# Down of two token blocks by seven half products: an attention and SwiGLU layer on one core

## The chip, the core and the metric

The kernel runs on one core of a Trainium2 chip. Five engines work side by side, each through its own list of instructions in order: TensorE (PE) multiplies matrices, VectorE (DVE) and ScalarE (ACT) work on rows, GpSimd (POOL) does little here, and SyncE (SP) issues nearly all DMA transfers. Semaphores order them where one needs another's result. The metric is the device time of one execution in microseconds (us), as the median of several runs.

## What is computed

`x` is 2048 tokens of 640 features, fp32. The reference, cut to what matters:

```python
q, k, v = (layernorm(x) @ wqkv) split into 32 heads of 20
logits  = q[s] . k[s - 2*w] * 20**-0.5  for w = 0..7      # sliding window of 8, step 2
h       = x + (softmax(logits) @ v) @ wo
g, u    = silu(layernorm(h) @ w_gate), layernorm(h) @ w_up    # 640 -> 1728
out     = h + (g * u) @ w_down                            # 1728 -> 640
```

Gate and Up are the products with `w_gate` and `w_up`; Down is the one with `w_down`.

## The kernel before

The 2048 tokens are four blocks of 512 (numbered 0 to 3 in the code; here the first to the fourth), each of four tiles of 128 rows. Every fp32 product is made of three products of a faster format: each operand is split into a high part (a cast on ACT) and the low rest (a subtraction on DVE), and high x high, low x high and high x low are added up in one of eight banks of 128 x 512 in PSUM. The 1728 features of the feed-forward part are 14 F-tiles, the last of 64.

The program runs in stages that overlap. The projection to q, k, v (L580) of the blocks comes first; attention itself is DVE and ACT work with transfers through DRAM, spread over more than half of the span; the output projection `wo` (L827, matmuls of 320 columns) follows block by block. The first two blocks then run gate and up (L899, banks 5 and 6), and Down (L910): the four tiles of rows go into banks 0 to 3, 512 of the 640 output columns wide, and the other 128 columns, turned, into bank 4. `finish` copies bank 4 (L1197), turns it back by four transposes on TensorE (L1201), and adds the results to h (L1209, L1212).

The third and fourth block share gate and up: F-tiles p and p+6 form a pair, the two blocks are the other dimension, and the 2 x 2 product of halves is done by seven products in place of eight (L994, added up on DVE at L1137). `early` does what needs the third block alone, `pair` the rest: 78 matmuls a pair, in banks 5, 6 and 7. F-tiles 12 and 13 stay plain (L1016). Down of these two blocks is ordinary: each tile's 15 matmuls are put between the products of the next pair, and the third block's F-tiles p+6, kept until then (`stash`), are done at the end (`closing`).

Before gate and up stands a second norm, whose result must be turned so that features lie on partitions. Half of the columns of the first three blocks go by DVE transposes and a transfer out and back, the other half by TensorE (L447, added at L450); the fourth block goes by DVE and DRAM alone (L455, L457 to a DRAM tensor `ysc`, L463 back, L472).

Nothing of the order on an engine follows from the order of the code. Each operation is recorded with an engine, a guessed cost and a priority (`P.add`). `order` schedules the list several times (`ROUNDS`), each time with due times worked back from the round before, and sorts by start time; a table `SHIFT` moves single operations by so many microseconds. Each engine then issues its operations in that sequence, SP its transfers.

The head: DVE makes the statistics of the first tiles (L390 to L392), TensorE turns them (L541), ACT casts the columns (L543) and the weights (L554), DVE makes the low parts (L544, L556).

## Time and profile before

| what | value |
|---|---|
| median of 3 runs | 841.8 us (841.59 to 842.68) |
| the profiled execution | 841.39 us |
| its span, first to last instruction | 839.3 us |
| granted TensorE clock | 0.999 |
| ACT busy | 414.0 us, 49% |
| DMA moved | 198.32 MB, 236 GB/s |

The span is what the profile divides up; the 2.1 us between it and the run's time lie around the program. A row of a group gives the line, engine and operation, the tiles written and read, the shape and the count, then the busy time in us, the mean of one in ns, and the idle time ahead of them with what ended it. A matmul's own duration overlaps the next, so what one costs in a stream is read from stretches of them. A row of a stretch gives, for each engine, busy us and instructions, then the clock, the DMA share and GB/s.

### The profile page before, as it was taken

The numbers are of one execution on the slowest core, as the hardware profiler recorded it, in microseconds if no ns is written. First come the engines' busy times: TensorE is split into PE (matmuls) and PEld (weight loads), VectorE is DVE, ScalarE is ACT, GpSimd is POOL, SyncE is SP. The second block draws the span as 40 slices with busy tenths as digits, with TensorE's granted clock in tenths as the row PEclk, the third lists the DMA queues.
The fourth block names the chain that finished last, engine by engine and source line by source line (L and its number), as shares of the span: only waits on it lengthen the run. The fifth ranks groups of instructions, "written<-read, shape, count | busy, mean of one in ns | idle before, by whom it ended". The sixth has DMA issues, their size and how long they took to land.

```text
span 839.3 us, 10718 instructions
## 1 busy us (share of the span) xinstructions
PE 831.4 (99%) x3903; PEld 705.0 (84%) x3903; DVE 694.7 (83%) x823; ACT 414.0 (49%) x694; POOL 23.2 (3%) x33
## 2 busy tenths in 40 slices
PE   8999999999999999999999999999999999999998
PEld 7888888889978889888888988888887888888886
DVE  8599999999999999999999999996327866655552
ACT  7755853333763445755443486464465533323231
POOL 0000000000000000000000000000000000000000
PEclk9999999999999999999999999999999999999999
DMA  8996786568688687669898658787587644454441
GB/s 265 331 367 219 284 272 216 185 213 307 197 304 263 224 289 258 212 210 372 287 365 289 233 174 304 250 269 268 156 264 270 218 170 137 136 169 144 154 133 71
DMA packets 101796, 198.32 MB, mean 236 GB/s; under 512 B 35744, under 2 KB 61152, under 8 KB 101104
## 3 DMA queue, kind: packets, MB, share of 16 engines
q1 hardware_dynamic: 101744, 197.65, 69.6%
q8 instruction: 30, 0.49, 0.2%
q14 instruction: 22, 0.18, 0.1%
HBM read 147.87 MB, written 49.75 MB: 235 GB/s over the span
## 4 chain that ended last, share of the span: by engine, by line
PE 75%; DVE 15%; DMA 4%; issue 2%; ACT 2%; SPq 1%; DVEq 0%; ACTq 0%
PE bank L580 20%; PE bank L910 17%; PE bank L899 17%; PE bank L994 16%; PE bank L827 5%; DVE fa L629 2%; DVE fa L636 2%; DVE fa L672 2%; DVE fa L664 2%; DMA fa<-ysc 1%; DMA fa<-in_ffn_dram 1%; DMA ysc<-fa 1%; DVE fa L934 1%; DMA fa<-in_wqkv_dram 1%; DMA fa<-osc 1%
## 5 line engine op out<-in xcount | busy, mean ns | idle before, releaser
L899 PE MATMUL bank<-shb,ra 128*128 128x512 f32 x810 | 189.7, 390 | 1.1 <-DVE shb L450 1.1
L899 PEld LDWEIGHTS bank<-shb,ra 128*128 128x128 f32 x810 | 151.4, 188 | 32.4 <-DVE shb L450 1.5
L910 PE MATMUL bank<-ra,acts 128*128 128x512 f32 (+1 forms) x662 | 161.9, 389 | 0.2 <-DVE acts L945 0.2
L910 PEld LDWEIGHTS bank<-ra,acts 128*128 128x128 f32 x662 | 122.6, 188 | 25.5 <-DVE acts L945 0.5
L580 PE MATMUL bank<-ra,sha 128*128 128x480 f32 x480 | 105.1, 379 | 0.6 <-ACT sha L543 0.6
L580 PE MATMUL bank<-ra,shb 128*128 128x480 f32 x470 | 102.5, 378 | 0.0
L580 PEld LDWEIGHTS bank<-ra,sha 128*128 128x128 f32 x480 | 89.8, 188 | 14.5 <-ACT sha L543 0.9
L580 PEld LDWEIGHTS bank<-ra,shb 128*128 128x128 f32 x470 | 88.1, 188 | 13.2
L664 DVE TENSOR_TENSOR fa<-fa 128x2560 f32<-128x2560 f32 x32 | 90.2, 2820 | 0.6
L629 DVE TENSOR_TENSOR fa<-fa 128x2560 f32<-128x2560 f32 x32 | 90.1, 2816 | 0.8 <-DMA fa<-ksc 0.4
L636 DVE TENSOR_REDUCE fa<-fa 128x128 f32<-128x2560 f32 x32 | 90.0, 2814 | 0.4
L994 PE MATMUL bank<-shb,ra 128*128 128x512 f32 x360 | 86.8, 390 | 0.3 <-DVE fa L938 0.3
L1137 DVE TENSOR_TENSOR fa<-bank,fa 128x512 f32<-128x512 f32 x60 | 41.1, 691 | 52.8 <-PE bank L994 51.4
L994 PEld LDWEIGHTS bank<-shb,ra 128*128 128x128 f32 x360 | 67.2, 188 | 14.6 <-DVE fa L938 0.7
L672 DVE TENSOR_TENSOR fa<-fa 128x1280 f32<-128x1280 f32 (+2 forms) x70 | 76.7, 1095 | 1.1
L827 PE MATMUL bank<-ra 128*128 128x320 f32 x480 | 75.0, 310 | 0.0
L827 PEld LDWEIGHTS bank<-ra 128*128 128x128 f32 x480 | 72.1, 188 | 2.9 <-ACT fa L830 1.3
L585 ACT ACTIVATE st<-bank,fa 128x480 f32<-128x480 f32 x64 | 41.9, 656 | 57.2 <-PE bank L580 54.4
L994 PE MATMUL bank<-ra 128*128 128x512 f32 x288 | 68.2, 389 | 0.0
L944 ACT CAST acts<-fa 128x512 fp32r<-128x512 f32 x47 | 29.1, 620 | 71.9 <-DVE fa L934 50.3
L994 PEld LDWEIGHTS bank<-ra 128*128 128x128 f32 x288 | 54.1, 188 | 11.2
L876 ACT CAST ra<-fa 128x1280 fp32r<-128x1280 f32 (+1 forms) x38 | 45.8, 1205 | 24.1 <-PE bank L899 15.0
(146 smaller groups left out, 834.5 us busy)
## 6 DMA issues: line engine op xcount, KB each, us to landing
fa<-in_ffn_dram SPq DMA_DIRECT2D x46, 960.0 KB, 6.5
ra<-lsc SPq DMA_DIRECT2D x45, 320.0 KB, 3.0
fa<-ksc SPq DMA_DIRECT2D x16, 880.0 KB, 6.0
fa<-vsc SPq DMA_DIRECT2D x16, 880.0 KB, 6.9
ra<-lsc SPq DMA_DIRECT2D x21, 640.0 KB, 5.0
lsc<-ra SPq DMA_DIRECT2D x13, 640.0 KB, 3.2
ksc<-st SPq DMA_DIRECT2D x16, 320.0 KB, 2.8
qsc<-st SPq DMA_DIRECT2D x16, 320.0 KB, 3.6
```

Source lines behind the costliest of these rows:

```text
L580: T.matmul(banks[bk][:, 0:480], l, r_(wq(g, w, c), 480), start=(p, c) == first_mm, stop=(p, c) == last_mm)
L585: P.add("ACT", act(480) + 0.06, lambda bk=bk, j=j: A.activation(stage_t()[:, so : so + 1920].rearrange("p (t j c) -> p t j c", t=3, j=NJ)[ ...
L629: P.add("DVE", dve(2560), lambda: V.tensor_tensor(f(PROD, 2560).rearrange("p (j w c) -> p j w c", j=2, w=W), window(ko, 2 * jp), f(qo + 32 ...
L636: P.add("DVE", dve(2560), lambda: V.tensor_reduce(f(lo + 128 * jp, 128), f(PROD, 2560).rearrange("p (n d) -> p n d", d=DH), axis=AX.X, op= ...
L664: V.tensor_tensor(f(PROD, 2560).rearrange("p (j w d) -> p j w d", j=2, d=DH), bass.AP(tensor=fa[:, vo : vo + 160].tensor, offset=fa[:, vo ...
L672: V.tensor_add(dst(v), v[:, :, 0:m, :], v[:, :, m : 2 * m, :])
L827: T.matmul(banks[bk][:, 0:320], l, r_(m, 320), start=p == 0 and c == 0, stop=p == 2 and c == NC - 1)
L876: P.add("ACT", act(n), lambda: A.copy(r_(gu, n), f(raw, n)), r=[rf(raw, n)], w=[rr(gu, n)], prio=PR["fh"])
L899: T.matmul(banks[bk], r_(gu + 1280 * w + wid * c + col, 128), x2(a, c), start=p == 0 and c == 0, stop=p == 2 and c == NC - 1)
L910: T.matmul(banks[bk][:, lo:hi], l, m, start=first and p == 0, stop=last and p == len(passes) - 1)
L994: T.matmul(banks[bk], r_(ws[w] + 256 * q, 128), x(a, c), start=start and p == n == q == 0, stop=stop and p == 2 and n == len(terms) - 1 an ...
L1137: dv(0, lambda: V.tensor_add(fb(h, dst), banks[bk], fb(h, src)), [pb(bk)] + fr(h, src), fr(h, dst))
```

## The change

**Down of the third and fourth block.** With A11, A12 the gated F-tiles p and p+6 of the third block, A21, A22 those of the fourth, and B11 to B22 the matching halves of Down's weights (F-tile p or p+6, output columns 0 to 319 or 320 to 639), seven products P1 to P7 of 128-row tiles with 320 columns give all four quarters of the output. P1 is made in `early`, in banks 0 to 3 over all six pairs, and added to all quarters (`add_both`). The differences of weights are made on DVE after `early` (`down_combinations`), stored to DRAM with their low parts, and loaded again at the end (`turned_weights`, eight loads). A11 goes to DRAM; A21 + A22 and A22 stay on chip (`slot`), A12 as before. After the last pair `down_products` runs P4, P5, P6, P7, P2, P3, 72 matmuls each, in banks 0 to 3 and 4 to 7 by turns; DVE makes the operands' differences in place. The plain F-tiles 12 and 13 have their Down in 320 columns too.

**The norm.** TURN and HALF change: the second block's columns now go wholly by DVE and DRAM, the fourth's by TensorE (20 transposes, banks 7 and 4). `finish`, now only for the first two blocks, turns bank 4 by a DVE transpose and a transfer out and four back. Of the five small DVE operations that refine 1/sqrt, one goes to ACT, and so does a sixth that scaled the mean. `wo` of the fourth block takes banks 7 and 4.

**The head.** x's first tile comes in two halves, on SP's and ACT's queue, the other three tiles before any weight; its mean is made by ACT (256 columns) and DVE (384 columns) in `one_split`.

**The order.** ROUNDS, the priorities and SHIFT are new, the last with several hundred entries where it had fifty.

```diff
-TURN = (3,)
+TURN = (1,)
 TURNED = (3,)
-HALF = (0, 1, 2)
+HALF = (0, 2)
...
 SHIFT = {
-    26: 0.6, 31: -47, 34: -25.1, 35: -4.3, 39: -16.4, 42: 1.8, 53: -0.6, 118: 0.9, 136: -103.6, 214: 10.2, 241:
...
+    12.4, 208: 2.4, 209: -2.5, 210: 7.2, 219: 5.2, 222: 13.4, 223: -9.5, 226: -0.7, 232: -27.6, 248: 7.4, 251:
...
+            if js == (0,):
+                for a, (eng, E) in enumerate((("SP", Q), ("ACT", A))):
+                    P.add(eng, 0.4, lambda a=a, E=E: E.dma_start(
+                        fa[a:128:2, XR : XR + 640],
+                        x_in[0, 64 * a : 64 * a + 64, 0, :]), w=[("xh", a, a + 1)] if a else [rf(XR, 640)], prio=0, nbytes=nb(64, 2560))
                 return
             for j in js:
...
+                (st.one_split if j == 0 else st.one_dve if j < 3 else st.one)(j)
...
+            P.add("SP", 0.45, lambda: Q.dma_start(asc[p], f(so, 512)), r=[rf(so, 512)], w=[(f"A{p}", 0, 1)], prio=PR["js"], nbytes=nb(128, 2048))
+
+            def mm():
+                for j in range(NJ):
+                    for q, (a, w) in enumerate(((0, 0), (0, 1), (1, 0))):
+                        T.matmul(banks[j][:, 0:320], act_t()[:, ao + 512 * a + 128 * j : ao + 512 * a + 128 * j + 128], r_(dn[w], 320), start=p == q == 0, stop=p == NP - 1 and q == 2)
+            P.add("PE", 12 * 0.1475, mm, r=[("ab", ao, ao + 1024), rr(dn[0], 320), rr(dn[1], 320)], w=[pb(j) for j in range(NJ)], prio=10)
...
+        def plain_down(b, batch):
+            for n in range(2 * NJ):
+                j, o, bk = n % NJ, 320 * (n // NJ), n % 5 if b == 2 else 4
+
+                def mm(j=j, o=o, bk=bk):
+                    t = [(ao, dn, a, w) for i, ao, dn in batch for a, w in (((0, 0), (0, 1)) if i == NF - 1 else ((0, 0), (1, 0), (0, 1)))]
+                    for q, (ao, dn, a, w) in enumerate(t):
+                        T.matmul(banks[bk][:, 0:320], act_t()[:, ao + 512 * a + 128 * j : ao + 512 * a + 128 * j + 128], r_(dn[w] + o, 320), start=q == 0, stop=q == len(t) - 1)
+                P.add("PE", 5 * 0.1475, mm, r=[x for i, ao, dn in batch for x in (("ab", ao, ao + 1024), rr(dn[0], 640), rr(dn[1], 640))], w=[pb(bk)], prio=10)
+                add_row(b, j, o, bk)
+
+        def add_row(b, j, o, bk, prio=1.2):
+            row, key = hrow(b, j, o, 320)
+            P.add("DVE", dve(320), lambda: V.tensor_add(row(), banks[bk][:, 0:320], row()), r=[pb(bk), key], w=[key], prio=prio)
+
+        def add_both(b, j, bk):
+            row, key = hrow(b, j)
+            v = lambda: row().rearrange("p (h c) -> p h c", h=2)
+            P.add("DVE", dve(640), lambda: V.tensor_add(v(), banks[bk][:, 0:320][:, None, :].to_broadcast([128, 2, 320]), v()), r=[pb(bk), key], w=[key], prio=5)
```

```diff
+        def down_combinations(p):
+
+            raw, t = (PROD, SETS + 1024)[p % 2], PROD + 1280
+            for q, i in ((0, p), (1, p + NP)):
+                P.add("SP", 0.45, lambda q=q, i=i: Q.dma_start(f(raw + 640 * q, 640), ffn_in[i, :, 1280:1920]), w=rx(raw + 640 * q, 640), prio=PR["tp"], nbytes=nb(128, 2560))
+            B11, B12, B21, B22 = (raw + 320 * q for q in range(4))
+            for n, x, y in ((0, B12, B11), (1, B22, t), (2, B22, B12), (3, B21, t + 320)):
+                P.add("DVE", dve(320), lambda n=n, x=x, y=y: V.tensor_sub(f(t + 320 * n, 320), f(x, 320), f(y, 320)), r=rx(x, 320) + rx(y, 320), w=rx(t + 320 * n, 320), prio=PR["tp"])
+            for h in range(2):
+                o, src = 2048, t + 640 * h
+                P.add("ACT", act(640), lambda o=o, src=src: A.copy(act_t()[:, o : o + 640], f(src, 640)), r=rx(src, 640), w=[("ab", o, o + 640)], prio=PR["tp"])
+                P.add("DVE", dve(640), lambda o=o, src=src: V.tensor_sub(act_t()[:, o + 640 : o + 1280], f(src, 640), act_t()[:, o : o + 640].bitcast(F32)),
+                      r=rx(src, 640) + [("ab", o, o + 640)], w=[("ab", o + 640, o + 1280)], prio=PR["tp"])
+                P.add("SP", 0.45, lambda h=h, o=o: Q.dma_start(tsc[h, :, 1280 * p : 1280 * p + 1280], act_t()[:, o : o + 1280].bitcast(F32)),
...
+        def down_product(name, k, at_, bks, last=False):
+
+            ops = []
+            for p in range(NP):
+                a22, s1 = slot(2 * p + 1), slot(2 * p)
+                s2 = s1
+                src, key = {"P2": stash(p), "P3": s2, "P4": a22, "P5": s1, "P6": s2, "P7": a22}[name]
+                if name == "P6":
+                    o = SETS + 512 * p
+                    P.add("SP", 0.45, lambda p=p, o=o: Q.dma_start(f(o, 512), asc[p]), r=[(f"A{p}", 0, 1)], w=rx(o, 512), prio=PR["mld"], nbytes=nb(128, 2048))
+                    P.add("DVE", dve(512), lambda o=o, s1=s1: V.tensor_sub(s1[0](), s1[0](), f(o, 512)), r=[s1[1]] + rx(o, 512), w=[s1[1]], prio=PR["mx"])
+                if name == "P7":
+                    P.add("DVE", dve(512), lambda a22=a22, s2=s2: V.tensor_sub(a22[0](), a22[0](), s2[0]()), r=[a22[1], s2[1]], w=[a22[1]], prio=PR["mx"])
+                if name == "P3":
+                    a12 = stash(p)
+                    P.add("DVE", dve(512), lambda a12=a12, s2=s2: V.tensor_sub(s2[0](), a12[0](), s2[0]()), r=[a12[1], s2[1]], w=[s2[1]], prio=PR["mx"])
+                sp, o = RING[gn[0] % len(RING)]
+                gn[0] += 1
+                t = lambda a, n=512, c=0, sp=sp, o=o: (ra if sp == "ra" else shb)[:, o + 512 * a + c : o + 512 * a + c + n]
+                P.add("ACT", act(512), lambda t=t, src=src: A.copy(t(0), src()), r=[key], w=[(sp, o, o + 512)], prio=PR["mh"])
+                P.add("DVE", dve(512), lambda t=t, src=src: V.tensor_sub(t(1), src(), t(0).bitcast(F32)), r=[key, (sp, o, o + 512)], w=[(sp, o + 512, o + 1024)], prio=PR["ml"])
+                ws, wk = at_(p)
+                ops.append((p, t, ws, [(sp, o, o + 1024)] + wk))
```

```diff
+        def down_products():
+            low, high = (0, 1, 2, 3), (4, 5, 6, 7)
+            down_product("P4", 3, turned_weights(3, (16896, 7168)), low)
...
+            down_product("P5", 0, turned_weights(0, (0, 1920)), high)
+            for j in range(NJ):
+                add_row(2, j, 320, high[j])
+                add_row(3, j, 320, high[j])
+            down_product("P6", 1, turned_weights(1, (3840, 5760)), low)
+            for j in range(NJ):
+                add_row(2, j, 320, low[j])
+                add_both(3, j, low[j])
+            down_product("P7", 2, turned_weights(2, (7680, 9600)), high)
+            for j in range(NJ):
+                add_both(3, j, high[j])
+                store_row(3, j, 0, 640)
...
+            at_ = lambda h: lambda p: ((1280 * p + 320 * h, 1280 * p + 640 + 320 * h), [rr(1280 * p, 1280)])
+            down_product("P2", None, at_(0), low)
+            for j in range(NJ):
+                add_row(2, j, 0, low[j])
+                store_row(2, j, 0, 320)
+            down_product("P3", None, at_(1), high, last=True)
+            for j in range(NJ):
+                add_row(2, j, 320, high[j])
+                store_row(2, j, 320, 640, two=j == NJ - 1)
```

```diff
+        def finish(b):
+            so = AB2
+            P.add("ACT", act(512), lambda: A.copy(f(so, 512), banks[4]), r=[pb(4)], w=[rf(so, 512)], prio=0)
+            P.add("DVE", dve(512), lambda: V.transpose(f(so, 512), f(so, 512)), r=[rf(so, 512)], w=[rf(so, 512)], prio=PR["dt"])
+            P.add("SP", 0.45, lambda: Q.dma_start(dsc[b], f(so, 512)), r=[rf(so, 512)], w=[(f"D{b}", 0, 4)], prio=PR["dt"], nbytes=nb(128, 2048))
...
-        for i in range(2 * NP, NF):
-            step(plain(i, x2, shr))
+        plain_down(2, [plain(i, x2, shr) for i in range(2 * NP, NF)])
         for p in range(NP):
-            step(early(p), 2 if p == NP - 1 else 1)
-        wo(3, PR["w3"], (7,))
+            early(p)
+        for p in range(NP):
+            down_combinations(p)
+        wo(3, PR["w3"], (7, 4))
         ln2_columns(3, 1)
-        while pend:
-            downs([pend.pop(0)], False, not pend)
-        finish(2, store=False)
+        for j in range(NJ):
+            add_both(2, j, j)
+            add_both(3, j, j)
...
-        first[0] = True
-        for i in range(2 * NP, NF):
-            step(plain(i, x3, x3r))
+        plain_down(3, [plain(i, x3, x3r) for i in range(2 * NP, NF)])
+        P.add("POOL", 0.1, lambda: G.memset(slot_t()[:, 3838:3840], 0.0), w=[("ab", 0, 3840)], prio=0)
         for p in range(NP):
-            for t in pair(p):
-                step(t)
-        downs([pend.pop(0)], False, True)
-        finish(3)
-        fb = (6, 7, 0, 1, 5)
-        todo = [closing(p) for p in range(2)]
-        for n in range(NP - 2):
-            downs([todo.pop(0)], n == 0, False, fb, whole=n == NP - 3)
-            todo.append(closing(n + 2))
-        downs(todo, False, True, fb, cut=True)
-        finish(2, fb, final=True)
+            pair(p)
+        down_products()
```

How the order moves, at three places. First ACT at the start of the program: L308 and, in the change, L366 prepare the square root's table; L554 and L638 cast weights, L543 and L627 columns of x. Before:

```order
L308 ACT_TABLE_LOAD
L308 ACTIVATE fa_65<-fa_65 128x1 [waits DVE_49]
L554 CAST ra_66<-fa_65 128x480 [waits DMAHW2_49]
L543 CAST sha0_123<-bank7_75 128x512 [waits PE_49]
L543 CAST sha0_123<-bank5_73 128x128 [waits PE_49]
L554 CAST ra_66<-fa_65 128x480 [waits DMAHW3_49]
L554 CAST ra_66<-fa_65 128x480 [waits DMAHW4_49]
L543 CAST sha0_123<-bank6_74 128x512 [waits PE_49]
```

With the change, where L442 sums 256 columns of x's first tile, and L410 to L413 are statistics of its fourth:

```order
L593 DMA fa_65<-in_x_dram 64x640
L442 ACT_TABLE_LOAD [waits DMAHW1_49]
L442 ACTIVATE fa_65<-fa_65 128x256 [waits DMAHW0_49]
L366 ACT_TABLE_LOAD
L366 ACTIVATE fa_65<-fa_65 128x1 [waits DVE_49]
L627 CAST sha0_128<-bank7_75 128x128 [waits PE_49]
L627 CAST sha0_128<-bank6_74 128x512 [waits PE_49]
L410 ACTIVATE fa_65<-fa_65 128x640 [waits DMAHW3_49]
L411 ACTIVATE fa_65<-fa_65 128x1 [waits Activation_49]
L413 ACTIVATE fa_65<-fa_65 128x640 [waits Activation_49]
L638 CAST ra_66<-fa_65 128x480 [waits DMAHW5_49]
```

The first table load now has a wait on a transfer (x), a second load follows it, and the fourth tile's statistics stand ahead of the first weight cast.

Second, TensorE in the middle of a pair (L994 before, L1067 with the change, and Down's L910 before). Before:

```order
L994 MATMUL bank5_73<-ra_66 128x512 [waits DVE_49]
L994 MATMUL bank5_73<-ra_66 128x512 x8
L910 MATMUL bank4_72<-acts_1904,ra_66 128x512 x2
L910 MATMUL bank4_72<-acts_1904,ra_66 128x512 [waits DMAHW5_49]
L910 MATMUL bank0_68<-ra_66,acts_1904 128x512 x3
L994 MATMUL bank5_73<-shb_67,ra_66 128x512 [waits DVE_49]
L994 MATMUL bank5_73<-shb_67,ra_66 128x512 x8
L910 MATMUL bank1_69<-ra_66,acts_1904 128x512 x3
L910 MATMUL bank2_70<-ra_66,acts_1904 128x512 x3
L910 MATMUL bank3_71<-ra_66,acts_1904 128x512 x3
L910 MATMUL bank4_72<-acts_1904,ra_66 128x512 [waits Activation_49]
```

With the change:

```order
L1067 MATMUL bank5_73<-shb_67,ra_66 128x512 x8
L1067 MATMUL bank6_74<-ra_66 128x512 x2
L1067 MATMUL bank6_74<-ra_66 128x512 [waits DMAHW5_49]
L1067 MATMUL bank7_75<-ra_66 128x512 [waits Activation_49]
L1067 MATMUL bank7_75<-ra_66 128x512
L1067 MATMUL bank5_73<-ra_66 128x512 [waits DVE_49]
L1067 MATMUL bank5_73<-ra_66 128x512 x5
L1067 MATMUL bank7_75<-ra_66 128x512 x4
L1067 MATMUL bank5_73<-shb_67,ra_66 128x512 [waits DVE_49]
L1067 MATMUL bank5_73<-shb_67,ra_66 128x512 x5
L1067 MATMUL bank7_75<-shb_67,ra_66 128x512 [waits DVE_49]
```

Before, a use of bank 5 has Down's matmuls ahead of it, here six. Now it has products of banks 6 and 7, five ahead of one use and four ahead of another.

Third, TensorE at the first pair, where the plain tiles' Down (L1124) goes through bank 4 alone; before, Down stood there in banks 0 to 4 as in the rows above:

```order
L1124 MATMUL bank4_72<-ra_66,acts_1955 128x320 [waits DVE_49]
L1124 MATMUL bank4_72<-ra_66,acts_1955 128x320 x4
L1067 MATMUL bank7_75<-ra_66 128x512 [waits DVE_49]
L1067 MATMUL bank7_75<-ra_66 128x512 x2
L1124 MATMUL bank4_72<-ra_66,acts_1955 128x320 [waits DVE_49]
L1124 MATMUL bank4_72<-ra_66,acts_1955 128x320 x4
L1067 MATMUL bank7_75<-ra_66 128x512 x3
L1067 MATMUL bank7_75<-ra_66 128x512 [waits DVE_49]
L1067 MATMUL bank7_75<-ra_66 128x512
L1067 MATMUL bank7_75<-ra_66 128x512 [waits DMAHW6_49]
L1067 MATMUL bank5_73<-ra_66 128x512 x3
L1124 MATMUL bank4_72<-ra_66,acts_1955 128x320 [waits DVE_49]
```

Each group of five on bank 4 waits for DVE, which adds the group before to h; once only three products stand between.

247 lines of the change are left out of this document (131 added, 116 removed), and 59 rows, old and new, of the table SHIFT.

## The prediction

> **What bounds the kernel now.** I read the page first, then what TensorE waited for, the busy time by stretch, the chain of waits, and the groups by line with their shapes apart.
>
> ```profile
> span 839.3 us, 10718 instructions
> PE 831.4 (99%) x3903; PEld 705.0 (84%) x3903; DVE 694.7 (83%) x823; ACT 414.0 (49%) x694; POOL 23.2 (3%) x33
> ```
> ```profile
> PE bank L497 <- POOL ra L1239: 1.3, 1, 1.3
> PE bank L899 <- DVE shb L450: 1.1, 1, 1.1
> PE bank L580 <- ACT sha L543: 0.6, 1, 0.6
> PE bank L541 <- DVE fa L392: 0.5, 1, 0.5
> PE bank L910 <- DVE acts L945: 0.4, 2, 0.2
> PE bank L994 <- DVE fa L938: 0.3, 1, 0.3
> ```
> TensorE (PE) is busy 831.4 of 839.3 us and waits 4.2 us in all, 2.4 of them before its first products. So matmuls taken away shorten the span, unless their removal uncovers another engine. Which one, the stretches tell (PE, weight loads, DVE, ACT, POOL busy, clock, DMA share, GB/s):
>
> ```profile
> 236.00:316.00 80.00, 79.12 (x353) 65.76 (x354) 79.86 (x87) 34.09 (x43) 1.83 (x3) 1.00 0.80 267
> 470.00:602.00 132.00, 131.68 (x656) 112.41 (x655) 111.80 (x137) 74.46 (x120) 5.47 (x6) 1.00 0.72 237
> 602.00:660.00 58.00, 57.77 (x257) 47.34 (x256) 32.47 (x47) 33.67 (x49) 0.00 (x0) 1.00 0.78 260
> 660.00:815.00 155.00, 154.81 (x685) 127.60 (x684) 94.91 (x148) 54.28 (x94) 0.00 (x0) 1.00 0.43 145
> ```
> While attention lasts, DVE is full too (79.86 of 80 us) and still holds PE up little, because attention runs ahead. After 602 DVE has room: 25 us before 660, 60 us from 660 to 815. The change spends that room.
>
> **Fewer columns through TensorE.** The prices, from the chain (start, us, instructions back to back) and the groups:
>
> ```profile
> 314.69 2.19 PE bank L827 x15
> 350.22 3.40 PE bank L910 x15
> 829.65 0.44 PE bank L1201 x4
> ```
> ```profile
> L910 PE MATMUL bank<-ra,acts 128*128 128x512 f32 x650 | 160.4, 391 | 0.2 <-DVE acts L945 0.2
> L910 PE MATMUL bank<-acts,ra 128*128 128x512 f32 x164 | 46.8, 392 | 0.2 <-DVE acts L945 0.2
> L910 PE MATMUL bank<-ra,acts 128*128 128x256 f32 x12 | 1.6, 282 | 0.0
> L827 PE MATMUL bank<-ra 128*128 128x320 f32 x480 | 75.0, 310 | 0.0
> L827 PEld LDWEIGHTS bank<-ra 128*128 128x128 f32 x480 | 72.1, 188 | 2.9 <-ACT fa L830 1.3
> ```
> Back to back a 512-column matmul takes 3.40/15 = 0.227 us, a 320-column one 2.19/15 = 0.146, a transpose 0.44/4 = 0.11. Down has 650+164 = 814 matmuls of 512 columns. Each of the first two blocks keeps 13 F-tiles x 15 + 10 for the last = 205, so blocks three and four have 404 and the 12 of 256 columns: 404 x 0.227 + 12 x 0.13 (1.6/12) = 93.2 us. The change puts 584 of 320 columns there: 72 in the early P1, 80 for the plain tiles, 6 products x 72 = 432. 584 x 0.146 = 85.3 us. That is **−7.9 us**; with 0.147, since L827's runs are short, −7.3. I take −7.4. Of the transposes (L447 and L1201 among them) 78 become 68: −1.1. **PE work: −8.5 us.**
>
> [...]
>
> **The room on DVE.** Prices:
>
> ```profile
> L1137 DVE TENSOR_TENSOR fa<-bank,fa 128x512 f32<-128x512 f32 x60 | 41.1, 691 | 52.8 <-PE bank L994 51.4
> L672 DVE TENSOR_TENSOR fa<-fa 128x320 f32<-128x320 f32 x6 | 2.9, 490 | 0.1
> L893 DVE TENSOR_TENSOR ra<-fa,ra 128x640 fp32r<-128x640 f32 x40 | 31.7, 812 | 0.0
> ```
> Added are 24 weight differences of 320 columns and 12 low parts of 640 (24 x 0.49 + 12 x 0.81 = 21.5 us), 24 operand combinations of 512 (16.6), 18 more low parts (12.4), and wider additions of results in 320s and 640s (some 15): about 65 us, so DVE ends near 760 us busy. Reading the changed order with these durations, stage by stage: from attention's end to the first pair PE has 79 us of work and DVE about 67; in the six pairs 110 against 98; in the last products 65 against 50. DVE fits, at 77 to 89%. The weight differences lie where attention ends (470 to 660: 45.7 us of room for 21.5). If that cover were gone they would delay block four's output projection by what is over.
>
> Within a pair the cover shrinks:
>
> ```profile
> 664.95 15.64 PE bank L994 x69
> 688.30 15.64 PE bank L994 x69
> ```
> A pair now takes 23.35 us from one to the next, with Down's matmuls between its products. In the change nothing is between: 78 products, 17.7 us, against 22 DVE operations of 0.69 = 15.2. Bank 5 is refilled after only 5 and then only 4 products of other banks (1.13 and 0.91 us), where before it was never under 6 (1.36). A refill needs the last matmul's 0.39 us (0.16 beyond its 0.227) plus 0.69 for DVE's read plus some 0.07 of signalling: 0.92. So both are just met when DVE is free at that moment, and missed by up to 0.69 each when it has another operation in hand. Below nothing the cost cannot be; its bounds are 0 and 6 x 2 x 0.69 = 8.3 us. I take 0, because DVE's order puts exactly the reading addition there. At the first pair block four's plain tiles send eight sums through bank 4 alone, one refill of it after 3 products (0.68 us) for a turn that needs 0.74 (0.49 in place of 0.69), others after 8 and more, with DVE full there (about 22 us of work in 21.5): bounds 0, and 4 for six refills late by 0.69; I take **+1.0**.
>
> The weights of the last products are reloaded from DRAM, 8 loads issued one product (10.6 us) ahead; the longest landing among loads of that size is what the turn chain showed:
>
> ```profile
> 623.51 4.68 DMA ysc<-fa
> 628.34 8.24 DMA fa<-ysc
> 635.31 2.11 PE L910 MATMUL bank<-ra,acts 128*128 128x512 f32 x8 [0.23 <-DVE acts L945]
> ```
> 8.24 us fits, and P2's and P3's 12 loads have three products over them: nothing. The same rows show what else goes: block four's norm columns went by DVE and DMA, and the work behind them was late (0.23 here, the L910 row of 0.4 above). With that norm on TensorE the chain is gone. The two gaps are 0.4, plus 2 x 0.16 hidden in the drain of the matmul ahead: **−0.7**. The wait of L899 (1.1) I leave: block one's columns are late there after DVE work that starts with the head. Block two's columns now take the DMA route; they have some 56 us of PE work over them: nothing. Block one's and two's 128 odd columns of Down come back by one DVE transpose and DMAs (0.69 and, by the nearest rows, 5 to 13 us) with whole blocks of slack before h is stored: nothing.
>
> **The head.** The timeline before:
>
> ```profile
> 0.74 1.28 ACT L308 ACT_TABLE_LOAD   x1 [0.74 <-PEq L1365]
> 2.04 0.20 ACT L308 ACTIVATE fa<-fa 128x1 f32<-128x1 f32 x1
> 4.14 0.89 DVE L390 BATCH_NORM_STATS2 fa<-fa 128x6 f32<-128x320 f32 x2 [2.08 <-DMA fa<-in_x_dram]
> 6.40 0.59 ACT L554 CAST ra<-fa 128x480 fp32r<-128x480 f32 x1 [4.16 <-DMA fa<-in_wqkv_dram]
> 7.53 0.49 PE L580 MATMUL bank<-ra,sha 128*128 128x480 f32 x1 [0.55 <-ACT sha L543]
> 9.74 0.74 ACT L352 ACTIVATE fa<-fa 128x640 f32<-128x640 f32 x1
> 10.38 0.18 ACT L352 ACTIVATION_READ_ACCUMULATOR fa<-fa 128x1 f32 x1
> 10.60 0.20 ACT L353 ACTIVATE fa<-fa 128x1 f32<-128x1 f32 x1
> 10.84 0.83 ACT L355 ACTIVATE fa<-fa 128x640 f32<-128x640 f32 x1
> 13.86 165.46 PE bank L580 x766
> ```
> Before, the table load runs while x is on its way, and the first product stands at 7.53. In the change ACT's first table load waits for the first x tile itself. That tile comes in halves, so a little sooner: about 3.85. Then 1.28 for the load, 0.6 for ACT's sum (5.7); DVE's mean and 128 columns (6.0); meanwhile a second table load, 1.28, with its 0.2 (7.2); two casts (8.0); then ACT takes the fourth tile's statistics, the four rows from 9.74 on, 1.93 us long (9.95), and only then the first weight cast, 0.59: first product near 10.6. By then 11 of the 20 transposes are done; 9 transposes and 20 products of 0.216 (165.46/766) remain, 5.3 us: level at 15.9 where before it was 13.86. **Head +2.0.** Bounds: 0, if the table load does not wait and the weights land as early, and 3.1, if nothing of the lost time is filled.
>
> [...]
>
> **The tail:**
>
> ```profile
> 829.84 5.80 PE L910 MATMUL bank<-ra,acts 128*128 128x512 f32 x30
> 835.69 0.42 DVE h L1209
> ```
> Now one 256-column addition (0.42) stands behind the last matmul; then one of 320 (0.49), with three others that come a little faster than DVE adds: **+0.2**.
>
> **Sum.** 839.3 − 8.5 + 1.0 − 0.7 + 2.0 + 0.2 = 833.3 us of span. The profiled run took 841.39, 2.1 more than its span; the median shown, 841.8, is 2.5 more. 833.3 + 2.3 = **835.6 us**, 0.7% faster.
>
> **Rivals.**
> - *The head costs nothing* and no new gap opens. For: x is issued first, and in halves. Against: the order of ACT, where two loads and a tile's statistics stand ahead of the cast. 835.6 − 2.0 − 1.0, and the L899 gap gone (−1.1): 831.5.
> - *DVE's turn of banks becomes the bound*, in the place above: both short covers of each pair are missed because a 0.69 us operation is ahead (8.3 us), and the plain tiles' bank 4 costs 4 in place of 1 (3.0): 835.6 + 11.3 = 846.9, slower. It decides from about 0.65 of those misses on (843.5). For: 86% of a pair's time is DVE work, and the longest wait of L994 for DVE, 0.3, is one with Down's matmuls between the products. Against: from 236 to 316 DVE at full load cost PE one wait.
> - *The gain is eaten, no change*: one short cover of each pair missed (4.1 us) and the head at its bound (+1.1): 840.8.
> - *Loads pace the 320-column matmuls.* L827's loads take 72.1/480 = 0.150 us of engine time each, no less than the spacing; one load alone takes 0.188. If Down's loads do not overlap as L827's do: 584 x (0.188 − 0.146) = 24.5 us, 860. Against: L827 holds 0.146 with loads of the same shape.
>
> **Numbers.** Forecast 0.63, own range 832.8 to 838.8 (head 0 to 3.1, plain tiles 0 to 4, not all at once); head free 0.14; DVE 0.12; eaten 0.09; loads 0.02. Two runs of this kernel differ by up to 0.13%, so 0.2%, 1.7 us, is what can be told: faster is below 840.1, slower above 843.5. Faster 0.63 + 0.14 = 0.77 and a little of "eaten": 0.78; same 0.08; slower 0.14. Range 831.0 to 842.0: it leaves out most of the two slow cases and the lower half of the free head, 0.2 together.
>
> **What would show it.** Right: 584 matmuls of 320 columns in 85 us; PE's busy time near 823 us, its waits near 7 us, 3 of them before its first product, at about 10.6 us; DVE near 760 us. Wrong: a first product at 7.5 us or less; waits of the pairs' products for DVE's additions that add up to over 2 us; a spacing of the 320-column matmuls over 0.15; a wait of the last products for a DMA; attention's output projections of blocks two or four waiting for DVE. If PE waits over 15 us in all, the forecast falls.

## The result, and the profile after

| | before | after |
|---|---|---|
| median, same chip (14 runs each) | 842.44 us (841.53 to 845.99) | 842.21 us (840.34 to 844.87) |
| after to before | | 0.9996, 95% interval 0.9984 to 1.0008 |
| span of the profiled execution | 839.3 us | 842.1 us (run 843.94) |

No change that can be told, where 0.7% faster was forecast. The page after, span and busy time:

```profile
span 842.1 us, 11291 instructions
PE 828.3 (98%) x4061; PEld 713.9 (85%) x4061; DVE 754.7 (90%) x916; ACT 425.3 (51%) x742; POOL 25.5 (3%) x34
```

DVE's 754.7 is close to the 760 forecast. TensorE's busy 828.3 is not the 823, and 3 us under before instead of 8. What it waited for (us in all, times, longest):

```profile
PE bank L1067 <- DMA ra<-lsc: 1.6, 1, 1.6
PE bank L1067 <- ACT fa L1104: 1.6, 2, 1.1
PE bank L625 <- DVE sha L628: 1.4, 1, 1.4
PE bank L1067 <- ACT ra L1222: 1.3, 1, 1.3
PE bank L575 <- POOL ra L1417: 1.3, 1, 1.3
PE bank L983 <- ACT shb L527: 0.7, 1, 0.7
PE bank L560 <- ACT fa L1414: 0.6, 1, 0.6
```

Five of these rows are new: L1067, the pairs' products, waits for a load (`lsc`, low parts of weights) and, in two rows, for ACT; L625, the head's transposes, for DVE; L560, the fourth block's norm transposes, for ACT. No row of L1067 waits for DVE's additions, and none of L1315, the last products, waits for anything. The new waits of L1067 and L560 lie between 565 and 660 us, in `early` and at the start of the first pair. The same stretch by windows (TensorE, weight loads, DVE, ACT, POOL busy, clock, DMA share, GB/s), before and then after:

```profile
590.00:640.00 50.00, 49.77 (x240) 41.75 (x239) 16.83 (x31) 26.57 (x39) 0.00 (x0) 1.00 0.72 234
```
```profile
590.00:640.00 50.00, 47.75 (x253) 40.70 (x252) 31.00 (x63) 36.95 (x64) 0.00 (x0) 1.00 0.92 323
```

TensorE loses 2 us of 50 there while DVE is at 62% and ACT at 74%: neither is short of time. What rises to nearly full is the DMA share, 0.72 to 0.92. ACT's group of the casts L1147, which make the high parts of the weight differences, and ACT's timeline at the largest of the waits say who holds whom:

```profile
L1147 ACT CAST acts<-fa 128x640 fp32r<-128x640 f32 x12 | 8.7, 727 | 9.5 <-DMA tsc<-acts 7.2 <-DVE fa L1144 2.3
```
```profile
628.66 0.59 ACT L1104 COPY fa<-bank 128x512 f32<-128x512 f32 x1 [0.49 <-PE bank L1067]
...
634.61 0.72 ACT L1147 CAST acts<-fa 128x640 fp32r<-128x640 f32 x1 [2.51 <-DMA tsc<-acts]
635.24 0.58 ACT L1104 COPY fa<-bank 128x512 f32<-128x512 f32 x1
```

and TensorE's timeline and the chain of waits for the same moment:

```profile
633.93 0.86 PE L1067 MATMUL bank<-shb,ra 128*128 128x512 f32 x3
635.87 2.33 PE L1067 MATMUL bank<-shb,ra 128*128 128x512 f32 x9 [1.08 <-ACT fa L1104]
```
```profile
628.04 6.49 DMA tsc<-acts
```

All halves of the differences use one buffer. The cast L1147 may only write there when the store of the half before has left, and that store took 6.49 us; ACT stood still for 2.51, and the copy L1104, which has nothing to do with it but stands behind it on ACT and empties a bank for the pairs, came late. In all ACT waited 7.2 us for these stores.

For a ledger I took, for each matmul, the distance from its start to the next one's, and compared it with the median of its shape. What lies more than 0.25 us above is listed as a wait, by place. The time given here and below for the 100th, 300th or 480th product is the start of the one behind it:

| kernel | ratio to before | 480th q/k/v product at | waits 555–580 | 580–645 | 645–670 | last matmul's start to the end | span |
|---|---|---|---|---|---|---|---|
| before | | 113.1 | 0.5 | 0.5 | 0.4 | 3.9 | 839.3 |
| after | 0.9996 | 117.1 | 1.7 | 2.7 | 1.5 | 5.0 | 842.1 |
| e11_again | 0.9993 | 117.1 | 1.0 | 3.0 | 1.5 | 5.0 | 841.5 |
| e1_table | 0.9981 | 114.4 | 0.8 | 1.8 | 2.4 | 5.0 | 838.7 |
| e2_head | 0.9982 | 116.2 | 1.4 | 2.2 | 1.5 | 4.9 | 840.2 |
| e3_two | 0.9968 | 115.8 | 1.5 | 0.0 | 1.5 | 4.6 | 838.1 |
| e4_nostore | 0.9951 | 116.4 | 1.1 | 0.0 | 1.5 | 4.5 | 837.0 |
| e5_oldhead | 0.9987 | 117.1 | 0.6 | 1.4 | 2.1 | 5.0 | 840.7 |
| e6_order | 0.9985 | 116.0 | 2.7 | 2.1 | 1.9 | 4.4 | 841.6 |
| e7_nogather | 0.9978 | 116.6 | 0.4 | 2.0 | 2.1 | 4.8 | 841.3 |
| e8_all | 0.9954 | 114.6 | 0.3 | 0.4 | 2.4 | 4.1 | 836.7 |
| e9_gath | 0.9966 | 114.9 | 1.4 | 0.7 | 1.5 | 4.1 | 837.2 |
| e10_slot | 1.0044 | 116.8 | 0.7 | 1.3 | 1.7 | 4.9 | 844.7 |
| e12_best | 0.9970 | 113.6 | 1.4 | 0.9 | 1.5 | 4.1 | 837.6 |

From before to after, in the two profiles: matmuls −8.3 (404 of 512 columns at 0.227 and 12 of 256 at 0.12 go, 584 of 320 at 0.147 come: −7.3; ten transposes: −1.0), head +4.0, waits between 555 and 670 +4.6, end +1.1. Between 660 us and the end 18 intervals are 0.02 to 0.25 us too long, 1.4 us in all, against 5 and 0.4 before: +1.0. These make +2.4 of the +2.8. The rest lies in intervals under 0.25 us (14 from 580 to 645 add up to 1.5, 5 before to 0.5), less 0.4 by which the wait at the first gate product is shorter.

The ledger explains these two executions. The profiled run of the changed kernel, 843.94, is 1.7 us above its median, and the one before, 841.39, is 1.0 under; the medians themselves lie 0.2 apart the other way. Which terms vary from one execution to the next two profiles can't tell.

### The profile page after: what moved, and what is told of

Same layout as the page of the kernel before. It is cut to its first block, busy times and chain, and to the rows that moved or that the text cites. A ratio compares the mean times of both kernels' runs of the same rounds, so it can differ in the third digit from the quotient of the medians.

```text
span 842.1 us, 11291 instructions
## 1 busy us (share of the span) xinstructions
PE 828.3 (98%) x4061; PEld 713.9 (85%) x4061; DVE 754.7 (90%) x916; ACT 425.3 (51%) x742; POOL 25.5 (3%) x34
## 4 chain that ended last, share of the span: by engine, by line
PE 92%; DMA 4%; ACT 2%; DVE 1%; issue 0%; ACTq 0%
PE bank L664 25%; PE bank L983 22%; PE bank L1067 16%; PE bank L994 11%; PE bank L1315 7%; PE bank L911 7%; DMA tsc<-acts 3%; PE bank L1089 2%; PE bank L1124 1%; DMA ra<-lsc 1%; PE bank L1114 1%; DMA msc<-fa 1%; ACT acts L1147 0%; PE bank L625 0%; DVE acts L1148 0%
## 5 line engine op out<-in xcount | busy, mean ns | idle before, releaser
L983 PE MATMUL bank<-shb,ra 128*128 128x512 f32 x810 | 189.9, 390 | 0.7 <-ACT shb L527 0.7
L1067 PE MATMUL bank<-shb,ra 128*128 128x512 f32 x360 | 89.8, 395 | 3.2 <-DMA ra<-lsc 1.6
L1067 PEld LDWEIGHTS bank<-shb,ra 128*128 128x128 f32 x360 | 66.0, 188 | 19.4 <-ACT fa L1104 2.9
L994 PE MATMUL bank<-ra,acts 128*128 128x512 f32 x328 | 80.7, 390 | 0.0
L994 PEld LDWEIGHTS bank<-ra,acts 128*128 128x128 f32 x328 | 61.2, 188 | 12.5 <-DVE acts L1013 0.2
L1067 PE MATMUL bank<-ra 128*128 128x512 f32 x288 | 69.6, 391 | 1.3 <-ACT ra L1222 1.3
L1067 PEld LDWEIGHTS bank<-ra 128*128 128x128 f32 x288 | 53.7, 188 | 13.0 <-ACT ra L1222 1.7
L1017 ACT CAST acts<-fa 128x512 fp32r<-128x512 f32 x34 | 21.1, 620 | 46.1 <-DVE fa L1007 46.0
```

The lines of the kernel that those rows point to most:

```text
L983: T.matmul(banks[bk], r_(gu + 1280 * w + wid * c + col, 128), x2(a, c), start=p == 0 and c == 0, stop=p == 2 and c == NC - 1)
L994: T.matmul(banks[bk][:, lo:hi], l, m, start=first and p == 0, stop=last and p == len(passes) - 1)
L1067: T.matmul(banks[bk], r_(ws[w] + 256 * q, 128), x(a, c), start=start and p == n == q == 0, stop=stop and p == 2 and n == len(terms) - 1 an ...
```

## The experiments

Each kernel is the changed one with the edits named, timed against the kernel before on the same chip. Its order is kept except for the operations named; in some it is written out as a list of their numbers (`SEQUENCE`), which is not shown. Where an edit puts lines in, the numbers in its rows are shifted (the pairs' product, L1067 after, is L1161 in most of them), so the work is named beside them.

### The head: e1_table and e2_head

```diff
         order = P.order()
+
+        def after(n, m):
+            order.remove(n)
+            order.insert(order.index(m) + 1, n)
+        for n, m in [(2, 10)]:
+            after(n, m)
```

Operation 2 is L366, the first square root, on ACT; it goes right behind operation 10, ACT's issue of x's second half, and so ahead of the sum of x's first tile.

> One operation moved: the preparation of the square root's table (L366) goes ahead of the sum over x's first tile on ACT, so that the one table load does not wait for x. Theory (the head is set by ACT's queue): the second load goes too, the first transposes start 1.3 us sooner, at about 5.0 us, the first product at about 9.3 in place of 10.65 us, the 100th product near 33.7 in place of 35.0, and the run is 1 to 1.3 us shorter than the changed kernel. Rival (the head is set by transfers or by DVE's splitting of the weights): the first transposes move, the 100th product stays at 35.0, no gain.

842.0 us (840.51 to 844.85), 0.9981, interval 0.9965 to 0.9997. ACT's timeline of the changed kernel and of this one:

```profile
3.79 1.28 ACT L442 ACT_TABLE_LOAD   x1 [3.79 <-DMA fa<-in_x_dram]
...
5.61 1.28 ACT L366 ACT_TABLE_LOAD   x1
...
10.03 0.58 ACT L638 CAST ra<-fa 128x480 fp32r<-128x480 f32 x1
```
```profile
1.36 1.28 ACT L366 ACT_TABLE_LOAD   x1 [1.36 <-PEq L1533]
...
8.69 0.58 ACT L638 CAST ra<-fa 128x480 fp32r<-128x480 f32 x1
```

One load in place of two, and while x is on its way: the first weight cast comes 1.34 us sooner, the first product at 9.3 in place of 10.7, and the 480th at 114.4, 2.7 us sooner. That is more than the loads alone. The rest goes with the clock: from 6 to 14 us its mean is 1.00 here and 0.81 in the changed kernel (below).

e2_head added to this that the fourth tile's statistics stand behind the weight casts on ACT, and that the first weights are loaded ahead of x's last tiles:

```diff
+        for n, m in [(2, 10), (15, 9), (28, 15), (12, 28), (16, 12), (19, 16), (22, 19), (57, 55), (59, 129), (62, 59), (63, 62), (64, 63)]:
+            after(n, m)
```

> As the first, and the fourth tile's statistics on ACT and its transposes moved behind the first five weight casts, and the first four weight loads ahead of the fourth tile's load. Theory (ACT's queue): first product at 7.5 to 8.3 us, the 100th product near 31 to 31.5 us as in the kernel before, 3.5 to 4 us shorter than the changed kernel. Rival (splitting the weights on ACT and DVE sets the pace after the first product): first product early, but the 100th not under 33 us.

842.46 us, 0.9982 (0.9966 to 0.9997). The first product came at 9.2, but the 100th at 34.1, 1.8 later than in e1_table: TensorE waits 2.0 us at 5.8 for the tile's low parts on DVE, its next matmuls run under a granted clock of 0.50 from 9 to 11 us, and a wait of 0.9 opens at 18 us, where the tile that was put off is wanted. The statistics that stood ahead of the first weight cast are needed soon after; moving them moved the wait.

### The stores of the weight differences: e3_two and e4_nostore

```diff
+        def half(h, i, e):
+            if h == 0:
+                return act_t()[:, 2048 + i : 2048 + e]
+            return upper("kept", F32)[:, i:e].bitcast(F32R)
...
-                P.add("ACT", act(640), lambda o=o, src=src: A.copy(act_t()[:, o : o + 640], f(src, 640)), ...
+                P.add("ACT", act(640), lambda h=h, src=src: A.copy(half(h, 0, 640), f(src, 640)), ...
...
+        for n, m in [(1791, 1789)]:
+            after(n, m)
```

The last lines also issue one store of a finished output row (L1344) sooner on SP.

> Two buffers in place of one for the halves of Down's weight differences, so that the cast L1147 no longer waits for the store just before it. Theory (ACT stands behind the store, and what is queued on ACT behind the cast is late for TensorE): the waits of TensorE for ACT between 605 and 636 us (0.66, 0.78, 1.25 us of gaps) fall to under 0.8 in all, 2 to 2.5 us shorter than the changed kernel; the gaps at 565 (1.7) and 658 (1.5) stay. Rival (the transfers as such are too many): the gaps stay or move to waits for transfers, no gain.

840.89 us (839.82 to 842.27), 0.9968 (0.9954 to 0.9982): below the changed kernel's interval. The two groups of casts and the stretch, in this kernel:

```profile
L1152 ACT CAST kept<-fa 128x640 fp32r<-128x640 f32 x6 | 4.4, 728 | 0.0
L1152 ACT CAST acts<-fa 128x640 fp32r<-128x640 f32 x6 | 4.3, 725 | 2.0 <-DVE fa L1149 2.0
```
```profile
590.00:640.00 50.00, 49.91 (x268) 43.41 (x268) 33.39 (x65) 37.07 (x66) 0.00 (x0) 1.00 0.94 336
```

ACT no longer waits for a store, the waits from 580 to 645 us are gone (2.7 to 0.0), and TensorE is busy 49.91 of 50 us at a DMA share of 0.94. So it was not the DMA engines' load that held TensorE here but the cast's wait for the one buffer, with the copies behind it in ACT's queue. The waits at 565 and 655 us stay.

e4_nostore leaves the twelve stores out and loads other weights in their place:

```diff
-                P.add("SP", 0.45, lambda h=h, o=o: Q.dma_start(tsc[h, :, 1280 * p : 1280 * p + 1280], ...
+                P.add("SP", 0.45, lambda: None,
```

> Leaves out the 12 stores of Down's weight differences, and the eight loads at the end read other data of the same size, so the output of two blocks is wrong. Theory (ACT behind the store): as with two buffers, 2 to 2.5 us shorter, hardly more. Rival (the traffic of the stores slows other transfers): another 1 us or more beyond two buffers, with shorter landings of the other loads between 570 and 650 us.

839.14 us (838.84 to 839.77), 0.9951 (0.9931 to 0.9972). The same waits are gone, here without any change of order. The stretch from 590 to 640 us has a DMA share of 0.76, near before's 0.72: the stores are the added traffic there. That traffic costs something too, as the rival had it: e4 lies 1.7 us under e3 by the medians, and no run of the one reaches the other's. Loads of `lsc` issued from 570 to 650 us land in 3.9 us (median) in place of e3's 6.0. Of the 1.1 us between the two profiles 0.4 stand at 565; the rest is not located.

### The load at 565 us: e7_nogather and e9_gath

`lsc`'s load for the first pair's products in `early` is issued by SP in the midst of four gathers (L1384, `dsc`). They are `finish`'s: with them the second block's 128 odd columns of Down come back, turned. After:

```profile
559.13 1.32 SPq L1384 DMA_DIRECT2D fa<-dsc  x2
560.54 0.57 SPq L965 DMA_DIRECT2D ra<-lsc  x1
561.17 1.24 SPq L1384 DMA_DIRECT2D fa<-dsc  x2
```
```profile
564.59 1.07 PE L1067 MATMUL bank<-shb,ra 128*128 128x512 f32 x4
567.23 0.96 PE L1067 MATMUL bank<-shb,ra 128*128 128x512 f32 x3 [1.57 <-DMA ra<-lsc]
```

e7_nogather leaves the second block's trip out, its store and its four gathers:

```diff
-            P.add("SP", 0.45, lambda: Q.dma_start(dsc[b], f(so, 512)), ...
+            P.add("SP", 0.45, lambda: Q.dma_start(dsc[b], f(so, 512)) if b == 0 else None, ...
...
-                    dsc[b].rearrange("(d t) (j q c) -> q t j d c", t=32, j=NJ, q=4)[q]),
+                    dsc[b].rearrange("(d t) (j q c) -> q t j d c", t=32, j=NJ, q=4)[q]) if b == 0 else None,
```

> Leaves out the second block's trip through DRAM in the turning of Down's last 128 columns (one store, four small loads), so these columns of that block are wrong. Theory (these transfers, issued at 559 to 562.4 us, delay the load of the third block's first low weights, which TensorE waits for near 565 us): the gap of 0.8 to 1.7 us there falls under 0.4. Rival (that load is late because its buffer comes free late): the gap stays over 0.8.

841.32 us, 0.9978 (0.9968 to 0.9989). The wait for the load is gone: it is issued 0.9 us sooner and lands 5.1 us after its issue, in place of 6.7. 0.4 is left, for DVE:

```profile
564.24 1.52 PE L1161 MATMUL bank<-shb,ra 128*128 128x512 f32 x6
566.00 2.33 PE L1161 MATMUL bank<-shb,ra 128*128 128x512 f32 x9 [0.24 <-DVE fa L1105]
```

e9_gath keeps the gathers and issues L1384's four (operations 1779 to 1782) right behind the load L965 (operation 1838). With it go e1's order, e3's buffers and e6's last stores on two queues.

> The changed kernel with the square root's table first on ACT, two half buffers for the weight differences, the last stores spread over SP and ACT, and in addition the four gathers of the second block's finish issued on SP behind the load of the first lows instead of ahead of it. Theory (the lows L1067 waits for at 565 us land late because the gathers share the DMA engines with them; 1.1 to 2.7 us in the runs so far): the gap there falls below 0.5 us, no gap stays between 600 and 640 us but 0.2 each, the 100th q/k/v product stands near 32.3, and the time is 838.5 to 840 us, ratio to before 0.994 to 0.9965. Rival (it is the weight buffer's release at 560 us that sets the load, the gathers cost nothing): the gap stays at 1.3 us or more and the time is 840 to 841.

839.96 us, 0.9966 (0.9955 to 0.9976). The wait at 565 fell to 0.3, as the theory had it, but a new one of 1.1 us opened at 577:

```profile
576.70 0.60 PE L1005 MATMUL bank<-ra 128*128 128x320 f32 x3
578.27 2.02 PE L1005 MATMUL bank<-ra 128*128 128x320 f32 x12 [0.97 <-ACT ra L922]
```
```profile
573.37 0.62 ACT L922 CAST ra<-fa 128x512 fp32r<-128x512 f32 x1 [4.63 <-DMA fa<-osc]
```

The output projection's columns (`osc`), loaded next on SP, land at 573.0 and 573.3 us, no sooner than in the changed kernel (573.2); TensorE is now ahead and waits for them. DMA's queue line for this stretch, 555 to 580 us, in this kernel:

```profile
q1 hardware_dynamic: 5137, 8.08, 97.8%
```

The 16 engines are taken for 97.8% of it, and a change of order alone moved the wait and did not end it. A full queue is not new, it was 98.0% in this stretch before, with waits of 0.5; what is new is which transfers TensorE waits for.

### The first pair at 655 us: e6_order and e10_slot

In the changed kernel, as in most others, TensorE waits 1.5 us for the first combination of weights (L1222, cast by ACT). e6_order put that cast (operation 2235) ahead of ACT's L1010 (2205), which it stood behind. At the end of the kernel it finishes bank 5 second of the last four, and spreads the last stores over SP's and ACT's queues:

```diff
+            E = A if (b, o) == (2, 320) and j in (0, 2) else Q
...
-        order = P.order()
+        order = [int(n) for n in SEQUENCE.split()]
```

> Two places reordered, no work changed: at the first pair the cast L1222, which TensorE waits for next, goes ahead of the plain tile's silu L1010 on ACT, and at the end TensorE finishes bank 5 second and stores go out on SP and ACT by turns. Theory (order in ACT's queue, and SP's 0.55 us for each issue): the gap of 1.48 us near 655 us falls under 0.3, the end of the span comes 3.9 to 4.1 us after the last matmul in place of 4.65, together 1.5 to 2 us shorter. Rival (the cast waits for DVE's difference, not for its turn): the gap stays over 1 us.

842.08 us, 0.9985 (0.9976 to 0.9994). The wait became 1.05, with 0.58 and 0.30 behind it: nothing won there. It is the rival's sign, and ACT's row (the cast L1222 is L1316 here) names what the cast waits for, DVE's difference:

```profile
658.32 0.62 ACT L1316 CAST ra<-fa 128x512 fp32r<-128x512 f32 x1 [2.00 <-DVE fa L1315]
```

The end from the last matmul's start fell from 5.0 to 4.4 us.

e10_slot changed two things at once. The ring of combinations begins one place earlier, at a place that the products ahead don't read, and the first combination's three operations, DVE's difference among them, stand earlier in the order:

```diff
-        cn, dn_ = [3], [0]
+        cn, dn_ = [2], [0]
...
-        order = P.order()
+        order = [int(n) for n in SEQUENCE.split()]
```

> The changed kernel, but the ring in which the combinations of weights lie begins one place earlier (cn 2 in place of 3), so that the first combination goes to a place that the products before it don't read, and its three operations stand some 2 us earlier in the lists of DVE and ACT. Theory (the gap at 654 to 658 us in every run so far is the ACT cast of the first combination, which may only write when the last product of the stage before has read that place: a write after read, which the ring's phase alone decides): the gap of 1.0 to 1.5 us falls below 0.4, the time is 840.3 to 841.8, ratio 0.997 to 0.999. Rival (the cast waits for DVE's or ACT's queue or for the raw weights' load): the gap stays above 0.8 and the time is that of the changed kernel, 842.

846.58 us, 1.0044 (1.0029 to 1.0058). With the ring moved, operands of the last Down products (cast at L1306 after, L1400 here) are written ahead of products that still read the same places: the run computes something else, and TensorE waits 2.3 us at 761 for that cast. So its time tells nothing of the first pair; its rows there do:

```profile
655.94 2.20 PE L1161 MATMUL bank<-ra 128*128 128x512 f32 x9
657.98 0.60 PE L1218 MATMUL bank<-ra,acts 128*128 128x320 f32 x3
659.75 0.56 PE L1218 MATMUL bank<-ra,acts 128*128 128x320 f32 x2 [1.18 <-DVE acts L1107]
```

The first pair starts without a gap, and 2 us later TensorE waits 1.2 us for DVE's low part of the last plain tile (L1013 after), with 0.4 more behind it. DVE is nearly full there (18.64 of the 20 us from 640 to 660 after); what was put first pushed the other back. Whether the ring's place or the earlier difference ended the gap the run does not show. The wait can be moved, but no order tried here ended it; whether fewer DVE operations at that place would was not tried.

### The head of the kernel before: e5_oldhead, e8_all, e12_best

e5_oldhead grafts the first 150 operations of the order before, and its statistics of the first tile, onto the change:

```diff
-                (st.one_split if j == 0 else st.one_dve if j < 3 else st.one)(j)
+                (st.one_dve if j < 3 else st.one)(j)
-        order = P.order()
+        order = [int(n) for n in SEQUENCE.split()]
```

> The changed kernel with the head of the kernel before: x's first tile in one transfer, its statistics on DVE, and the first 150 operations in the order of the kernel before; all else stays in the changed kernel's order. Theory (the new head costs what the two profiles show): first product at 7.5 us, the 100th at 31.0 in place of 35.0 us, and 3 to 4 us shorter than the changed kernel. Rival (a late head is made up later, where TensorE waits for attention at 239 us): the 100th product at 31.0, but the wait before the first gate product grows from 0.9 by 2 us or more and the run is under 2 us shorter.

842.43 us, 0.9987 (0.9975 to 1.0). The 100th product came at 31.4 in place of 35.0, and the 480th at 117.1, as after: the 3.6 us were given back, and not at the rival's place, where the wait stays 0.9, but almost all at one other:

```profile
39.80 11.62 PE L752 MATMUL bank<-ra,sha 128*128 128x480 f32 x53
53.21 3.31 PE L752 MATMUL bank<-ra,sha 128*128 128x480 f32 x8 [1.79 <-DVE ra L728]
```
```profile
54.00:55.00 1.00, 1.00 (x4) 0.87 (x3) 0.93 (x4) 0.92 (x2) 0.00 (x0) 0.50 1.01 420
55.00:56.00 1.00, 1.00 (x4) 0.80 (x4) 0.97 (x3) 1.00 (x3) 0.00 (x0) 0.50 0.99 384
```

TensorE, now ahead of the new order that follows, waits for a weight's low part (1.8 us, behind two DVE operations of 2.8 and two short ones), and then eight products take 0.40 us each in place of 0.22 under a clock of 0.50.

e8_all put this head, e3's two buffers, e6's swap and its stores together:

> The old head, the two buffers and the two reorderings together. Theory (the loss is the sum of separate places): TensorE's gaps over 0.15 us add up to about 4 us as in the kernel before (3.8) against 10.8, and the run is 7.5 to 9 us shorter than the kernel before: 833.5 to 835.5. Rival (one removed wait uncovers the next): under 5 us shorter, with new gaps.

839.93 us (838.97 to 840.46, 5 runs), 0.9954 (0.9942 to 0.9967): 0.5% under before, half of what was expected, and so the rival's case. It has the lowest ratio beside e4_nostore, which leaves work out, though e9's and e12's intervals overlap it. Its wait at 51 us is 1.1, without the half clock, and 0.4 is left from 580 to 645.

e12_best took e8_all without the swap at the first pair, and moved that weight's two operations (L638, L640) 4 us earlier in the order.

> A version put together from what the runs before showed: the head of the kernel before (its order of the first 150 instructions), two half buffers for the weight differences, the last stores spread over SP and ACT, and the low half of one q/k/v weight split (L640 of the fourth group's third tile, and ACT's cast of its high half) taken some 4 us earlier, so that the product at 51 us need not wait for it. Theory (the change's products are worth 8.5 us and only the waits around them ate that): the wait at 51 us is gone, the 300th q/k/v product stands near 74.6 as in the kernel before (74.2), some 0.4 us stays in waits between 600 and 640 us, 1.0 to 2.7 at 565 and 1.5 at 654; time 838 to 840 us, ratio to before 0.993 to 0.996. Rival (the wait at 51 us has another cause behind it, or the gain is lost again later): the 300th product stays past 75.5 and the time is 840 or more.

840.03 us (838.91 to 843.65), 0.9970 (0.9958 to 0.9983). The wait at 51 us is gone, and the 300th product at 74.7, near the 74.2 before. The 1.0 us won there was lost again further on: against e8_all, the waits between 230 and 245 us are 1.0 longer and the one for the load at 564 is 1.2 longer. The two kernels' intervals overlap: ending the wait at 51 us brought nothing that can be told.

### The kernel once more: e11_again

> The changed kernel itself once more, profiled and timed a second time. Theory (the waits between 560 and 660 us and the later head are the program's; the granted clock's fall to a half behind a wait of 1.5 us or more is the execution's): the waits return at the same places with 0.3 us of play, the 100th q/k/v product stands at 33.3 to 35.1, the half clock may come at other places or none, and the time is 841.5 to 843 us, ratio 0.9985 to 1.0005. Rival (the waits are chance as well): other places, sizes that differ by over 1 us in all.

842.58 us, 0.9993 (0.9983 to 1.0003). The waits returned at the same places, and the 480th product at 117.1: they belong to the program. Their sums agree (555 to 645: 4.0 against 4.4; 645 to 670: 1.5), but single ones differ by more than the 0.3 expected, at 565 by 0.7 (1.0 against 1.7) and at 634 by 0.5 (1.7 against 1.2).

## Why the prediction was wrong

**Right.** The price of the columns: matmuls of 320 columns follow each other by 0.147 us in 1,062 cases, Down's −7.3 against −7.4 forecast, the transposes' −1.0 against −1.1. The weight loads, 0.188 us long each (L1315), did not hold them at that. The first product, 10.65 against 10.6. DVE's load. DVE's turn of banks did not become the bound: behind 660 us it costs at most the 1.0 us of small intervals, in place of the 0 that I took, from 0 to 8.3. (My own sum had the shorter cover at 0.91 us against 0.92 needed. Two other sums are off, and neither moves the forecast: the turn of bank 4 needs 0.72, not 0.74, and the rival of the banks decides from 0.70 of the misses, not 0.65. The 0.07 of signalling in these turns no run shows: in the trace before, DVE starts 0.04 us behind the end of the matmul it waits for, the median of 41 waits, and TensorE 0.05 behind DVE's, of 5. Together that is 0.09, 0.02 more a turn.) The plain tiles' bank 4, taken at 1.0, shows no wait over 0.25. The last products, with their reloaded weights, wait for nothing. The norm's two gaps went too, though its transposes (L560) got one of 0.6 in their place, behind ACT's queue.

**Head: +2.0 forecast, +4.0 measured.** Its mechanism was right, two table loads and a tile's statistics ahead of the first weight cast; the size was not. My 2.0 assumed that after 10.6 us the stream runs level at its usual speed. It ran at half speed until 14 us: from 11 to 14 the granted clock was 0.50, products took 0.40 us each in place of 0.22 and transposes 0.21 in place of 0.11. The window from 6 to 14 us, before and after:

```profile
6.00:14.00 8.00, 7.44 (x43) 6.27 (x44) 7.45 (x17) 7.41 (x17) 0.00 (x0) 1.00 0.99 341
```
```profile
6.00:14.00 8.00, 6.04 (x25) 4.60 (x26) 7.44 (x18) 7.47 (x18) 0.00 (x0) 0.81 0.87 303
```

A mean clock of 0.81 over 8 us is at most 1.5 us of lost work. Together with the delay of the first product it exceeds even the bound of 3.1 that I gave, which had no slower clock in it.

**The weight differences: nothing forecast, 2.2 measured.** This is the step that failed: the work and the transfers put where attention ends were to cost nothing, and cost 2.2 here and up to 1.2 in the next point. "DVE fits, at 77 to 89%", I wrote, and "The weight differences lie where attention ends (470 to 660: 45.7 us of room for 21.5)". DVE did fit. I priced the busy time of one engine and not the order of another. The cast goes through ACT, ACT takes its queue in order (the copy at 635.24 us came behind the cast at 634.61), and one buffer between the cast and a store of 4.7 to 7 us (the four in the chain of waits) makes ACT stand, 7.2 us in all; behind it stand copies that empty TensorE's banks. The experiments with two buffers and without the stores show it: in both the waits there fall from 2.7 to 0.0. (The 0.5 of before in that stretch is one of the norm's two gaps, which went.) The 1.7 us by which e4_nostore lies under e3_two say that the stores' traffic costs something beside.

**The second block's 128 odd columns of Down by DMA: "with whole blocks of slack before h is stored: nothing"; 0.5 and 1.2 measured** in the two profiles of the changed kernel (waits of 1.0 and 1.7 from 555 to 580, less before's 0.5), and up to 2.2 in the others. I asked who waits for the gathers' result, and nobody does. The cost fell on another transfer of the same queue, which took the 16 engines for 93.3% of the time from 555 to 580 us: the load of the first pair's low parts. e7_nogather shows that this trip causes it, with a landing in 5.1 us in place of 6.7; e9_gath that with the gathers behind the load this wait falls to 0.3 and one of 1.1 opens at 577. The second block's norm, which I also put at nothing, shows no wait of TensorE.

**The first pair: +1.0 forecast, +1.1 measured, by luck.** The forecast looked at bank 4 there, and found DVE full. DVE is full, but the wait came at the first combination's cast, of which I had no term. In e6_order that cast waits for DVE's difference; in e10_slot, with the difference and the ring's place moved, the gap goes and DVE's order takes it back at once.

**The tail: +0.2 forecast, +1.1 measured.** I counted DVE's last addition and left out how the stores behind it are issued. The last rows on DVE and SP, after, and SP's of before:

```profile
836.17 1.81 DVE L1130 TENSOR_TENSOR h<-bank,h 128x320 f32<-128x320 f32 x4 [8.75 <-PE bank L1315]
836.69 1.19 SPq L1344 DMA_DIRECT2D out_dram<-h  x2
...
838.61 0.56 SPq L1344 DMA_DIRECT2D out_dram<-h  x1
```

```profile
832.24 4.46 SPq L1217 DMA_DIRECT2D out_dram<-h  x4
```

An issue took 0.55 to 0.6 us of SP in the rows after. Before, the last one ended at 836.70, 1.3 us behind the last matmul's start (835.37); now at 839.17, 2.0 behind it (837.14), because the last row's store stands behind the others'; the other 0.4 us lie behind the last issue. With two stores moved to ACT's queue, the end is 4.4 us long in e6_order, and 4.1 in three others.

So the gain of the columns came whole. By the ledger 4.0 of it went into the head, 4.6 into waits between 555 and 670 us that the new work brings through ACT's, DVE's and the DMA's queues, 1.0 into small intervals of the pairs and 1.1 into the end, in an execution 1.7 us above the median. With the head, the buffer and the stores mended, e8_all kept some 3.9 us of it (0.46% of 842). What stays lost is the first pair's wait, which no run ended without opening another, and whichever of the waits at 51, 235 and 565 us the order leaves.

## What to carry to other kernels

When work goes into idle time, price each engine it passes by the place in its queue and not by room alone: here a cast that had to wait for a store to leave a single buffer held everything behind it on ACT, 7.2 us in all, and a second buffer gave back some 0.28%. Where the DMA engines are near full (93 to 98% from 555 to 580 us here), ask of every added transfer which load it delays, not only who waits for it. And a faster head gains only what the stream behind it can keep: e5_oldhead was 3.6 us ahead at 31 us and level with it by 78.
